# Attention and MLP on one core: row maxima turned by VectorE in 32 x 32 blocks and carried through DRAM instead of turned by TensorE

## The chip, the cores and the metric

One core of a Trainium2 chip runs the whole program. The metric is the device time of one execution in microseconds; of several executions the median is taken. The granted TensorE clock was 1.000 over the profiled execution.

## The reference

One transformer layer, sequence S = 2048, width D = 512, H = 32 heads of 16, MLP width F = 1792. First `h = x + softmax(q k^T / 4) v wo`, with q, k, v from `layernorm(x) @ wqkv`; then `h2 = h + silu(layernorm(h) @ w1) @ w2`:

```python
scores = jnp.einsum("bhqd,bhkd->bhqk", q, k) * scale
p = _softmax(scores, axis=-1)
o = jnp.einsum("bhqk,bhkd->bhqd", p, v)
...
h = x + _A_ref(_layernorm(x, axis=-1), A_wqkv, A_wo)
h2 = h + _B_ref(_layernorm(h, axis=-1), B_w1, B_w2)
```

The softmax needs the maximum of each query's 2048 scores before its exponentials can be taken.

## The kernel before

**Items and groups.** Attention is cut into 32 *items*: four heads by 512 queries each. Item i has 16 *groups* (one per 128 keys), so there are 512 groups, g = 16 i + c, walked in order by the main loop (L1244). A group is four score matmuls of 64 x 512 (`scores`, L451, keys as weights), each followed by an exponential on ScalarE (`pt<-ps`), and the four value matmuls in fp32 of the group two before (`values`, L815). Scores sit on one half of TensorE's rows, and between them stand up to three *maximum* matmuls on the other half (`maximum`, L273: 128 queries by 512 keys, 48 rows deep), each reduced over its 512 keys by VectorE (L289, `mx<-ps`). The maxima in group g serve items that come later; how many are done beside a group is decided by `maxima(g)` (L1221), normally three, two where c = 2.

**Where the other maxima are done.** An item has 64 maxima. Those of the first items are done beside the q, k, v projections; after each block of eight items (at g = 144, 272, 400, the `marks`) an MLP of the 512 finished rows runs as one piece (`mlp`, L1041), with *bursts* of maxima between its matmuls: pairs on both row halves, reduced two at a time (L287). Constants say how many: `BURSTS_1` in the first product, `BURSTS_2 = 16, 15, 13` bursts of four in the second, and `BESIDE = (138, 134, 106)` tells the planner the total per MLP. The last MLP stands after the last item.

**From maxima to scores.** When the last maximum of an item is recorded, `found_maxima` (L379) is called. `finish_max` (L296) takes the maximum over the four key blocks, either *urgent* by one VectorE reduction (L303, `nm<-mx`) or by six small GpSimd operations, and splits it in two halves of fp16 (`ns`, 128 queries x 32). `place_max` (L326) turns `ns` with a TensorE transpose into a PSUM bank of the ring `sm` (the three banks of the maxima), VectorE copies it out to `mt` (ScalarE before attention begins), and two DMAs of SyncE write `mt` to rows 48 and 49 of each half of the item's `qs`, so that the score matmuls subtract the maximum themselves. Scores of an item can't begin before that has landed.

**When.** `due_at` (L371) picks the step: where the item starts far enough ahead, the next group with c = 2 (`JOINT`; the previous item's result `pvs` is copied out of PSUM by VectorE there, L843); otherwise `WAIT` = 2 groups later. In the group that is due, `place_max` stands after the four scores and before the values (L1303). Outside attention, and near the marks, it is called by the agenda three steps later (`tick`, L356).

**Queues.** Each engine works through its instructions in program order, SyncE also: all DMAs here but the early weight loads are issued by SyncE, and a DMA that waits holds up those behind it. Per item SyncE carries eight loads of q and k for the item four ahead (L1250), the item's sums to DRAM and back (`dn`, `rc`, `dr`, `den`, L847 to L916) and, in the first items, weights to be split.

Of the kernel before, what the change touches and what calls it, by code (L numbers as in the profile page):

```python
# [12 lines left out]
F16 = mybir.dt.float16  # L13
# [7 lines left out]
P = 128  # L21
# [9 lines left out]
KC = S // P  # L31
# [21 lines left out]
RING = 5  # L53

HEADS = [(0, 1), (0, 0), (1, 1), (1, 0)]
ITEMS = NB * H // 4
# [5 lines left out]
FIRSTS = 8, 16, 24  # L62


WAIT = 2
JOINT = 2
AHEAD = 4


BESIDE = (138, 134, 106)  # L70
OUTPUT = 9

BESIDE_V = [(0, 0), (0, 4, 4, 4)], [(2, 2), (4, 4, 4, 4)], [(6, 6), (6, 6, 6, 6)]
# [5 lines left out]
BESIDE_A1 = 10, 9, 8, 7  # L79

BURSTS_1 = ({f: 6 for f in range(FC) if f not in (6, 13)},) * 2 + ({f: 6 for f in range(FC) if f % 3},)
BURSTS_2 = 16, 15, 13
SPAN_2 = 12 * (FC - 2)

MORE = 2, 2, 0
# [3 lines left out]
def attention_mlp_kernel(ctx: ExitStack, tc: tile.TileContext, x, wqkv, wo, w1, w2, out):  # L89
# [8 lines left out]
    def tr(*a):  # L98
        tc.keep_in_program_order(nc.tensor.transpose(*a))  # L99


    def pool(op, *a, **k):
        tc.keep_in_program_order(getattr(nc.gpsimd, op)(*a, **k))  # L103


    def pin(ins):
        tc.keep_in_program_order(ins)

    def act(fn, *a, **k):
        pin(getattr(nc.scalar, fn)(*a, **k))  # L110

    def dve(fn, *a, **k):
        pin(getattr(nc.vector, fn)(*a, **k))  # L113

    def dma(*a):
        pin(nc.sync.dma_start(*a))  # L116
# [22 lines left out]
    dram = ctx.enter_context(tc.tile_pool(name="dram", bufs=1, space=DRAM))  # L139
    small = ctx.enter_context(tc.tile_pool(name="small", bufs=3))  # L140
# [22 lines left out]
    def bank(kind="st", dtype=F32):  # L163
        ps = space[:, next_bank(kind), :]
        return ps if dtype == F32 else ps.bitcast(dtype)[:, :512]
# [32 lines left out]

    dn = dram.tile([H, 4, 512], F32, name="dn")
    dr = dram.tile([H, 4, 512], F32, name="dr")  # L200

    wd = {kind: dram.tile([FC, P, 2, 512], F16, name=f"{kind}d") for kind in ("w1", "w2")}

# [25 lines left out]
    ks, qs = [None] * RING, [None] * RING  # L229
# [37 lines left out]
    def start_of(piece):  # L267
        i, a = piece
        return KC * i + HALF * (a or 0)
# [3 lines left out]
    def maximum(i, kb, qt, a, j, n):  # L273

        piece = piece_of(i, a)
        width = 1 if i == LAST else 2
        if piece not in mx:
            mx[piece] = small.tile([P, 64], F32, name="mx", bufs=RING + 1)[:, :32 * width].rearrange(
                "p (j a q k) -> p j a q k", j=2, a=width, k=4)
            left[piece] = 32 * width  # L280
        heads = (0, 1) if j is None else (j,)
        for m, h in enumerate(heads):
            mm(space[:, n + m, :], qs[i % RING][64 * h:64 * h + 48, a, qt * P:qt * P + P],
               ks[i % RING][64 * h:64 * h + 48, a, kb * 512:kb * 512 + 512], start=True, stop=True)
        of = mx[piece][:, :, a % width, qt, kb]
        if j is None:
            pin(nc.vector.tensor_reduce(of, space[:, n:n + 2, :], axis=AX.X, op=ALU.max))  # L287
        else:
            pin(nc.vector.tensor_reduce(of[:, j:j + 1], space[:, n, :], axis=AX.X, op=ALU.max))  # L289
        left[piece] -= len(heads)  # L290
        at["done"] += len(heads)
        finish_rest()
        if left[piece] == 0:
            found_maxima(piece)

    def finish_max(piece, urgent):  # L296

        m4 = mx.pop(piece).rearrange("p j a q k -> p (j a q) k")
        rows = m4.shape[1]
        nm = small.tile([P, 16], F32, name="nm")[:, :rows]  # L300
        sign = 1.0
        if urgent:
            pin(nc.vector.tensor_reduce(nm, m4, axis=AX.X, op=ALU.max, negate=True))  # L303
        else:
            sign = -1.0
            m1, m2 = m4[:, :, :2], m4[:, :, 2:]
            for to, a, b in ((m2, m1, m2), (nm, m2[:, :, 0], m2[:, :, 1])):

                pool("tensor_tensor", to, b, a, ALU.subtract)
                pool("tensor_scalar", to, to, 0.0, None, op0=ALU.max)  # L310
                pool("tensor_tensor", to, to, a, ALU.add)
        ns = small.tile([P, 32], F16, name="ns")[:, :2 * rows]
        high, rest = (ns.rearrange("p (j r a) -> p j r a", j=2, r=2)[:, :, r, :] for r in range(2))
        nm = nm.rearrange("p (j a) -> p j a", j=2)
        pool("tensor_scalar", nm, nm, sign / MX, None, op0=ALU.mult)
        pool("tensor_copy", high, nm)
        pool("tensor_tensor", rest, nm, high, ALU.subtract)
        split[piece] = ns

    placed, split, unfinished, found_at = set(), {}, [], {"step": 0}  # L320

    def finish_rest():
        while unfinished:
            finish_max(unfinished.pop(), True)

    def place_max(piece):  # L326

        i, a = piece
        ns = split.pop(piece)
        n = ns.shape[1]  # L330
        ps = bank("sm", F16)
        tr(ps[:n, :P], ns, ident_h)
        mt = small.tile([32, P], F16, name="mt")[:n]
        if at["attention"]:
            dve("tensor_copy", mt, ps[:n, :P])
        else:
            act("copy", mt, ps[:n, :P])
        for j in range(2):
            dst = qs[i % RING][64 * j + 48:64 * j + 50, slice(None) if a is None else slice(a, a + 1)]
            dst = dst.rearrange("r a n -> r (a n)").rearrange("r (a b) -> r a b", b=P)  # L340
            pin(nc.sync.dma_start(dst, mt[n // 2 * j:n // 2 * (j + 1), :]))
        placed.add(piece)
# [6 lines left out]
    at = {"item": 0, "done": 0, "half": 0, "step": 0, "due": 0, "attention": False, "group": None, "ready": 0, "next": 0, "blocks": True}  # L349
    agenda, late = {}, {}  # L350

    def soon(steps, fn, *a):

        agenda.setdefault(at["step"] + steps, []).append((fn, a))
# [11 lines left out]
    def next_item():  # L366
        while at["item"] < ITEMS and not (todo[at["item"], 0] or todo[at["item"], 1]):
            at["item"] += 1
        return at["item"]

    def due_at(piece):  # L371

        g = at["group"]
        if g is None:
            return WAIT + 1
        joint = g + WAIT + (JOINT - g - WAIT) % KC
        return joint - g if joint < start_of(piece) - 2 and joint // KC - 1 not in (-1, *FIRSTS) else WAIT

    def found_maxima(piece):  # L379
        steps = due_at(piece)  # L380
        g = at["group"]
        if g is None or g + 1 in marks:
            soon(steps, place_max, piece)
            finish_max(piece, g is not None)
            return
        late.setdefault(at["step"] + steps, []).append(piece)
        if steps == WAIT:
            unfinished.append(piece)
            found_at["step"] = at["step"]
        else:  # L390
            finish_max(piece, False)

    def one_max(half=None, n=None):

# [32 lines left out]
    def burst(n, *pairs):  # L427
        assert n % 2 == 0
        for m in range(n // 2):
            two_max(pairs[m] if pairs else next_pair())  # L430
# [32 lines left out]
    with ExitStack() as pa:  # L463
# [320 lines left out]
        for g in range(1, NG // 2):  # L784
            for m, (b, key) in enumerate([(b, 1) for b in range(NB)] + [(b, 0) for b in range(NB)]):
# [3 lines left out]
                n = 8 * g + m - 12  # L789
# [251 lines left out]
    def mlp(b):  # L1041
# [9 lines left out]
        def some_scores(n):  # L1051
            for _ in range(n):
                scores(*ahead.pop(0), "sm")
# [22 lines left out]
        acc = []  # L1076
        inserts = {SPAN_2 * (n + 1) // BURSTS_2[b]: lambda: burst(4, 4, 6) for n in range(BURSTS_2[b])}
        inserts[12 * (FC - 2) + 8] = inserts[12 * (FC - 1) + 2] = lambda: some_scores(3)
# [140 lines left out]
    marks = [KC * (8 * b + 1) for b in range(1, NB)]  # L1219

    def maxima(g):  # L1221

        i, c = divmod(g, KC)
        goals = [(64 * (n + 1), KC * n) for n in range(i + 1, LAST)]
        goals += [(END - 32 * (1 - a), KC * LAST + HALF * a) for a in range(2) if KC * LAST + HALF * a > g]
        ready = min(ITEMS, i + RING - (0 if c == KC - 1 else 1)) * 64
        rate = max([(n - sum(x for x, m in zip(BESIDE, marks) if g <= m <= start) - at["done"])
                    / max(1, start - AHEAD - g) for n, start in goals] or [0])
        if ready < END:
            rate = min(rate, (ready - at["done"]) / (KC - 1 - c or KC))  # L1230
        at["due"] += max(0, rate)
        if g < LAG or g in marks or g - 1 in marks:

            return 0
        at["ready"] = ready
        most = 2 if c == JOINT and i and i - 1 not in FIRSTS else 3
        n = max(0, min(most, int(at["due"]), ready - at["done"]))
        at["due"] -= n
        return n
# [4 lines left out]
    for g in range(groups):  # L1244
        tick()
        i, c = divmod(g, KC)
# [13 lines left out]
        if i in FIRSTS:  # L1260
            b, n = i // 8 - 1, c - OUTPUT
# [20 lines left out]
        if g == 1:  # L1282
            dve("memset", pv, 0.0)
        at["group"] = g
        n = maxima(g)

        half = 1 - head(g, g % 2)[1]
        j = next_item()
# [58 lines left out]
```

## Time and profile before

| what | value |
|---|---|
| median of 3 runs | 1611.84 us (1611.49 to 1612.39) |
| profiled execution, its own time | 1613.29 us |
| profiled execution, span from first to last instruction | 1611.5 us |
| TensorE matmuls busy | 1590.8 us, 99% |
| VectorE busy | 1392.9 us, 86% |
| ScalarE busy | 1210.3 us, 75% |
| GpSimd busy | 456.4 us, 28% |
| granted TensorE clock | 1.000 |

A row of the timeline gives the start in us from the span's beginning, the duration, the engine, the line of the kernel, the operation, what it writes and reads, the partitions and elements, and how many equal instructions follow each other; in brackets the engine's idle time ahead of it and what ended it. Value matmuls (`ps<-pt,va`) come once per group, eight records of them, so the distance of two such rows is the time of one group. Line 96 is the helper through which all matmuls go, line 99 that of transposes, lines 103, 110, 113 and 116 those of GpSimd, ScalarE, VectorE and DMA issues.

### The profile page before, as it was taken

The numbers are of one execution on the slowest core, as the hardware profiler recorded it, in microseconds if no ns is written. First come the engines' busy times: TensorE is split into PE (matmuls) and PEld (weight loads), VectorE is DVE, ScalarE is ACT, GpSimd is POOL, SyncE is SP. The second block draws the span as 40 slices with busy tenths as digits, with TensorE's granted clock in tenths as the row PEclk, the third lists the DMA queues.
The fourth block names the chain that finished last, engine by engine and source line by source line (L and its number), as shares of the span: only waits on it lengthen the run. The fifth ranks groups of instructions, "written<-read, shape, count | busy, mean of one in ns | idle before, by whom it ended". The sixth has DMA issues, their size and how long they took to land.

```text
span 1611.5 us, 28300 instructions
## 1 busy us (share of the span) xinstructions
PE 1590.8 (99%) x10553; PEld 477.9 (30%) x10553; DVE 1392.9 (86%) x2060; ACT 1210.3 (75%) x2387; POOL 456.4 (28%) x702
## 2 busy tenths in 40 slices
PE   9999999999999999999999999999999999999998
PEld 6433222222233322222233322222233322222253
DVE  7899999999989889999989889999976789999421
ACT  6545799999964179999964179999964089999732
POOL 4743544544326101211136101211126101111100
PEclk9999999999999999999999999999999999999999
DMA  5668533342322111121223211121123111100222
GB/s 194 181 162 234 139 85 90 110 140 85 101 63 99 60 52 33 37 60 33 51 73 99 60 52 33 38 59 33 50 75 108 50 52 38 33 11 22 73 85 72
DMA packets 100949, 125.89 MB, mean 78 GB/s; under 512 B 24144, under 2 KB 61072, under 8 KB 100812
## 3 DMA queue, kind: packets, MB, share of 16 engines
q1 hardware_dynamic: 96204, 115.71, 25.1%
q10 hardware_dynamic: 4608, 8.39, 1.9%
q8 instruction: 82, 1.34, 0.3%
q14 instruction: 55, 0.45, 0.1%
HBM read 93.45 MB, written 24.63 MB: 73 GB/s over the span
## 4 chain that ended last, share of the span: by engine, by line
PE 85%; DVE 6%; ACT 4%; DMA 2%; issue 1%; POOL 1%; SPq 1%; DVEq 0%; ACTq 0%; POOLq 0%
PE ps L96 84%; ACT pt L110 4%; DVE mx L289 2%; DVE mx L287 2%; PE ps L99 1%; DMA qd<-sh 1%; DVE ot L113 1%; SPq L116 1%; DMA qs<-mt 0%; DVE st L113 0%; DMA ks<-in_A_x_dram 0%; DVE htl L113 0%; DVE hx L113 0%; POOL ri L103 0%; DVE pvs L113 0%
## 5 line engine op out<-in xcount | busy, mean ns | idle before, releaser
L110 ACT ACTIVATE pt<-ps 128x512 f32<-128x512 f32 x2048 | 1011.3, 631 | 154.9 <-PE ps L96 153.4
L289 DVE TENSOR_REDUCE mx<-ps 128x1 f32<-128x512 f32 x1474 | 926.8, 683 | 44.9 <-PE ps L96 16.1
L96 PE MATMUL ps<-qs,ks 64*128 64x512 f16 x2048 | 533.6, 379 | 5.8 <-DMA qs<-mt 2.5
L96 PE MATMUL ps<-pt,va 128*17 128x512 f32 x4096 | 537.5, 598 | 0.6
L96 PE MATMUL ps<-ks,qs 48*128 48x512 f16 x2048 | 494.7, 380 | 1.8 <-DVE mx L287 1.8
L287 DVE TENSOR_REDUCE mx<-ps 128x2 f32<-128x1024 f32 x287 | 334.0, 1219 | 55.1 <-PE ps L96 54.1
L96 PEld LDWEIGHTS <-ks 64*128 64x128 f16 x2048 | 150.8, 95 | 553.0 <-issue 433.2
L103 POOL TENSOR_TENSOR ri<-rc,minus 128x16 f32<-128x16 f32 x31 | 90.7, 2925 | 294.8 <-DMA rc<-dn 294.8
L96 PE MATMUL ps<-w,gh 128*128 128x512 f16 x672 | 157.4, 380 | 0.5 <-ACT g L110 0.4
L96 PEld LDWEIGHTS <-qs 48*128 48x128 f16 x2048 | 125.1, 94 | 75.3 <-issue 61.9
L96 PE MATMUL ps<-hth,w 128*128 128x512 f16 (+1 forms) x472 | 132.9, 369 | 0.0
L96 PEld LDWEIGHTS ps<-pt,va 128*17 128x17 f32 x4096 | 68.9, 95 | 214.6 <-issue 201.1
L110 ACT ACTIVATE g<-ps,factors 128x512 f32<-128x512 f32 x56 | 38.6, 689 | 124.6 <-PE ps L96 102.9
L96 PEld LDWEIGHTS <-w 128*128 128x128 f16 x708 | 66.1, 98 | 79.1 <-issue 11.8
L103 POOL TENSOR_TENSOR mx<-mx 128x32 f32<-128x32 f32 x36 | 8.6, 239 | 281.8 <-DVE mx L289 216.6
L96 PEld LDWEIGHTS <-gh 128*128 128x128 f16 x672 | 61.1, 98 | 85.5 <-issue 19.8
L96 PE MATMUL ps<-htl,w 128*128 128x512 f16 (+1 forms) x236 | 83.9, 368 | 0.0
L103 POOL TENSOR_SCALAR nm<-nm 128x16 f32<-128x16 f32 (+1 forms) x51 | 12.9, 254 | 169.8 <-DVE nm L303 154.5
L110 ACT ACTIVATE ks<-ps 128x512 f32<-128x512 f32 x30 | 18.0, 599 | 50.3 <-PE ps L96 37.6
L113 DVE SCALAR_TENSOR_TENSOR gh<-g,factors,gh 128x512 f16<-128x512 f32 x14 | 10.5, 751 | 52.2 <-ACT gh L110 52.2
L103 POOL TENSOR_TENSOR sl<-ks,sh 128x512 f16<-128x512 f32 x30 | 35.3, 1178 | 52.9 <-ACT sh L110 38.5
L103 POOL TENSOR_TENSOR gh<-g,gh 128x512 f16<-128x512 f32 x42 | 48.5, 1154 | 3.5
(153 smaller groups left out, 983.5 us busy)
## 6 DMA issues: line engine op xcount, KB each, us to landing
ks<-kd SPq DMA_DIRECT2D x120, 192.0 KB
w<-w1d SPq DMA_DIRECT2D x56, 256.0 KB
w<-w2d SPq DMA_DIRECT2D x56, 256.0 KB
ks<-in_B_w_dram ACTq DMA_DIRECT2D x28, 256.0 KB
w<-in_B_w_dram SPq DMA_DIRECT2D x28, 256.0 KB
qs<-qd SPq DMA_DIRECT2D x128, 48.0 KB
kd<-sh SPq DMA_DIRECT2D x16, 256.0 KB
qd<-sh SPq DMA_DIRECT2D x16, 256.0 KB
```

The source lines that it names most:

```text
L96: tc.keep_in_program_order(nc.tensor.matmul(*a, **k))
L99: tc.keep_in_program_order(nc.tensor.transpose(*a))
L103: tc.keep_in_program_order(getattr(nc.gpsimd, op)(*a, **k))
L110: pin(getattr(nc.scalar, fn)(*a, **k))
L113: pin(getattr(nc.vector, fn)(*a, **k))
L116: pin(nc.sync.dma_start(*a))
L287: pin(nc.vector.tensor_reduce(of, space[:, n:n + 2, :], axis=AX.X, op=ALU.max))
L289: pin(nc.vector.tensor_reduce(of[:, j:j + 1], space[:, n, :], axis=AX.X, op=ALU.max))
```

## The change

A second way to place an item's maxima, `place_far`, is added. `ns` (128 x 32) is turned by one VectorE transpose, which works on blocks of 32 x 32: row 32 b + c of `mt` then holds column c for the queries 32 b to 32 b + 31. Four DMAs write the four blocks side by side into a DRAM tensor `md` (32 x 128 per item, 64 bytes at a time), and two DMAs read it back, 16 rows of it as two rows of 1024, into the item's `qs`. `found_maxima` takes this way outside attention, near the marks, and for every whole item that starts more than `FAR` = 8 groups later; inside attention it is called `CALM` = 6 steps later, at the head of a group, and the maximum over key blocks is then always taken by GpSimd. Other items go as before, two groups later, with VectorE's urgent reduction; `due_at` is gone. In a group that is to hold a TensorE transpose, at most two maxima are done. The third MLP has 14 bursts in its second product instead of 13, and the planner is told 110 instead of 106.

In the instruction streams of the two built kernels this comes to: TensorE transposes of `ns` 33 before, 6 after; VectorE block transposes 0 and 27, copies of `mt` 30 and 6 (`mn`), urgent reductions 13 and 4; ScalarE copies of `mt` 3 and 0; small GpSimd operations 54 more; SyncE DMAs 108 more. Single reductions 1474 and 1482, pairs 287 and 283.

```diff
+FAR = 8
+CALM = 6
-BESIDE = (138, 134, 106)
+BESIDE = (138, 134, 110)
-BURSTS_2 = 16, 15, 13
+BURSTS_2 = 16, 15, 14
...
+    md = dram.tile([ITEMS, 32, P], F16, name="md")
...
+    def place_far(piece):
+        i, _ = piece
+        mt = small.tile([P, 32], F16, name="mt")
+        dve("transpose", mt, split.pop(piece))
+        for b in range(4):
+            dma(md[i, :, 32 * b:32 * b + 32], mt[32 * b:32 * b + 32, :])
+        for j in range(2):
+            dma(qs[i % RING][64 * j + 48:64 * j + 50].rearrange("r a n -> r (a n)"),
+                md[i, 16 * j:16 * j + 16, :].rearrange("(r q) n -> r (q n)", r=2))
+        placed.add(piece)
...
-        mt = small.tile([32, P], F16, name="mt")[:n]
-        if at["attention"]:
-            dve("tensor_copy", mt, ps[:n, :P])
-        else:
-            act("copy", mt, ps[:n, :P])
+        mt = small.tile([32, P], F16, name="mn", bufs=1)[:n]
+        dve("tensor_copy", mt, ps[:n, :P])
...
-    def due_at(piece):
-        g = at["group"]
-        if g is None:
-            return WAIT + 1
-        joint = g + WAIT + (JOINT - g - WAIT) % KC
-        return joint - g if joint < start_of(piece) - 2 and joint // KC - 1 not in (-1, *FIRSTS) else WAIT
-
-    def found_maxima(piece):
-        steps = due_at(piece)
+    def found_maxima(piece):
         g = at["group"]
-        if g is None or g + 1 in marks:
-            soon(steps, place_max, piece)
-            finish_max(piece, g is not None)
+        marked = g is not None and g + 1 in marks
+        if g is None or marked or piece[1] is None and start_of(piece) - g > FAR:
+            soon(WAIT + 1 if g is None or marked else CALM, place_far, piece)
+            finish_max(piece, marked)
             return
-        late.setdefault(at["step"] + steps, []).append(piece)
-        if steps == WAIT:
-            unfinished.append(piece)
-            found_at["step"] = at["step"]
-        else:
-            finish_max(piece, False)
+        late.setdefault(at["step"] + WAIT, []).append(piece)
+        unfinished.append(piece)
+        found_at["step"] = at["step"]
...
-        most = 2 if c == JOINT and i and i - 1 not in FIRSTS else 3
+        most = 2 if at["step"] in late or c == JOINT and i and i - 1 not in FIRSTS else 3
```

## The prediction

> **What bounds the kernel now.** I read the page first, then the timeline of TensorE, group by group, then VectorE, GpSimd and SyncE at the places where the change acts.
>
> ```profile
> PE 1590.8 (99%) x10553; PEld 477.9 (30%) x10553; DVE 1392.9 (86%) x2060; ACT 1210.3 (75%) x2387; POOL 456.4 (28%) x702
> PEclk9999999999999999999999999999999999999999
> PE 85%; DVE 6%; ACT 4%; DMA 2%; issue 1%; POOL 1%; SPq 1%; DVEq 0%; ACTq 0%; POOLq 0%
> ```
>
> TensorE is busy 99% of the span at full clock, and the chain that ends last runs 85% through it. So a microsecond taken from TensorE, or from its waits, counts. What one transpose costs there is read not from its own duration, since matmuls overlap, but from the distance of its neighbours. Value matmuls come once per group, so two such rows are one group apart.
>
> ```profile
> L113 DVE COPY mt<-ps x30: 197/200/213, 215.8 to 1494.1; 32x128 f16<-32x128 f16 x28, 16x128 f16<-16x128 f16 x2
> 1107.12 1.05 PE L96 MATMUL ps<-pt,va 128*17 128x512 f32 x8
> 1109.08 1.05 PE L96 MATMUL ps<-pt,va 128*17 128x512 f32 x8
> 1111.27 0.22 PE L99 MATMUL ps<-ident_h,ns 128*32 128x128 f16 x1 [0.16 <-DVE mx L289]
> 1111.28 1.06 PE L96 MATMUL ps<-pt,va 128*17 128x512 f32 x8
> 1097.26 1.05 PE L96 MATMUL ps<-pt,va 128*17 128x512 f32 x8
> 1099.28 1.05 PE L96 MATMUL ps<-pt,va 128*17 128x512 f32 x8
> 1065.84 1.05 PE L96 MATMUL ps<-pt,va 128*17 128x512 f32 x8
> 1067.86 1.05 PE L96 MATMUL ps<-pt,va 128*17 128x512 f32 x8
> ```
>
> The time of a group is very regular: 1.96 us (1107.12 to 1109.08). The group with the transpose at 1111.27 takes 2.20, 0.24 more; the transpose waits for the bank of a maximum, as its bracket says. At c = 2 a group takes 2.02 without a transpose (1097.26 to 1099.28) and 2.02 with one (1065.84 to 1067.86): there the values wait for VectorE's copy of `pvs`, and the transpose costs nothing. So of the transposes in attention only those away from c = 2 are worth anything.
>
> **The change part by part.** The sum is a difference: durations come from the profiled execution, whose span is 1611.5 us and whose own time is 1613.29; I take it from the median, 1611.84. Which item goes which way is counted through the two programs' loops: 27 of 33 pieces go far; items 8, 16, 24, 30 and the halves of 31 stay with TensorE.
>
> (1) *Single transposes away from c = 2 that go:* items 6, 7, 15, 23, 29. 5 x 0.24 = **1.2 us less**. Those that stood at c = 2 give nothing.
>
> (2) *Urgent reductions that go:* VectorE's `nm<-mx` in attention costs TensorE nothing or a tenth, by where it falls.
>
> ```profile
> 1108.11 0.39 PE L96 MATMUL ps<-qs,ks 64*128 64x512 f16 x1
> 1108.41 0.21 DVE L303 TENSOR_REDUCE nm<-mx 128x16 f32<-128x64 f32 x1
> 1151.23 0.21 DVE L303 TENSOR_REDUCE nm<-mx 128x16 f32<-128x64 f32 x1
> 1150.54 1.05 PE L96 MATMUL ps<-pt,va 128*17 128x512 f32 x8
> 1152.61 1.05 PE L96 MATMUL ps<-pt,va 128*17 128x512 f32 x8
> ```
>
> The one at 1108.41 stands ahead of a group's first reduction, and its group (1107.12 to 1109.08) is not longer. The one at 1151.23 stands ahead of a group's last reduction: 2.07 instead of 1.96, 0.11 more. Of those that go, items 6, 7, 14, 15 and 28 are of the costly kind: 5 x 0.11 = **0.55 less**. GpSimd gets nine times six small operations; it is busy 28% and has six groups for them, nothing.
>
> (3) *VectorE's block transposes come.* The trace has none. Lower bound nothing; nearest rows are the copy of `mt` and `nm<-mx`, 0.20 and 0.21 us, on as many values; I take 0.2. In attention they stand at the head of a group, exactly where the 0.21 us reduction cost nothing. Two fall in a group c = 1, ahead of the `pvs` copy: between 0 and 0.11 each, **0.1 more** together. The Trainium skill, "VectorE: DVE Perf Modes", section "The three transpose paths", gives 311 ns for VectorE on 128 x 128 bf16, and says that it turns 32 x 32 blocks only; by 0.31 instead of 0.2 the term would be 0.2. No run here shows it yet.
>
> (4) *The way through DRAM.* Four stores, a wait until they have landed, two loads.
>
> ```profile
> 383.41 0.33 SPq L116 DMA_DIRECT2D dr<-ri  x1
> 385.24 0.84 SPq L116 DMA_DIRECT2D den<-dr  x2
> 710.20 0.35 SPq L116 DMA_DIRECT2D rc<-dn  x1
> 711.83 2.93 POOL L103 TENSOR_TENSOR ri<-rc,minus 128x16 f32<-128x16 f32 x1 [8.52 <-DMA rc<-dn]
> ```
>
> A store of 64-byte pieces and the load behind it are 1.83 us apart (383.41 to 385.24), two issues take 0.84, a small load is used 1.63 after its issue (710.20 to 711.83). The block transpose ends about 0.5 us into its group (the reduction at 1108.41 starts 0.30 after its group's first scores at 1108.11). So: last store issued at 0.5 + 3 x 0.42 = 1.8, loads at 3.6 and 4.05, landed at 5.7, or 5.9 if the load is like a `qs<-mt` (below). Items 7 and 23 have the least time: found at c = 7 of the item before, called six groups later, 3 groups = 5.88 us ahead of their first scores. Items 15 and 29 have 4 groups, 7.84, the others more. I take 0.1 for each of 7 and 23, **0.2 more**; bounds 0 and 1.2 each (chain of 7.1). The Trainium skill, "DMA: Bandwidth & Descriptors", section "Anatomy of one DMA — SWDGE (gpsimd) path", puts about 2.0 us fixed on each DMA, mostly the write receipt, for GpSimd's queue; at 2.0 for each hop the chain would be 6.25 and the term 0.75. The store's row, 1.83, speaks for less.
> SyncE is held for some 4 us per item. Behind it stand loads of q and k for the item four ahead, weights loaded five ahead, and `pvs` sums that only GpSimd awaits: nothing.
>
> (5) *Items that stay, with two maxima in the transpose's group.*
>
> ```profile
> 428.83 0.20 DVE L113 COPY mt<-ps 32x128 f16<-32x128 f16 x1
> 429.06 1.38 SPq L341 DMA_DIRECT2D qs<-mt  x2
> 429.75 1.05 PE L96 MATMUL ps<-pt,va 128*17 128x512 f32 x8
> 432.61 1.05 PE L96 MATMUL ps<-pt,va 128*17 128x512 f32 x8
> 425.80 3.11 DVE L289 TENSOR_REDUCE mx<-ps 128x1 f32<-128x512 f32 x5
> ```
>
> Item 8: the copy to `mt` runs behind the group's third reduction, its DMAs land about 1.8 us after the second issue, and the group after takes 2.86 (429.75 to 432.61): 0.9 of waiting. Items 24 and 30 are the same. With two maxima the copy comes one reduction earlier, 0.6 us (3.11 for five): 3 x 0.6 = 1.8 less. For item 24 the urgent reduction moves to a free place (0.11 less), for item 30 to a dear one (0.11 more). The first half of item 31 saves 0.15 of its 0.24, since the transpose finds a free bank. Item 16 loses: one maximum fewer at item 8 makes it complete a group later, so that it is placed two groups ahead instead of three and has a wait of 0.3, and a dear reduction of 0.11. Together **1.5 less**; bounds 0.5 and 3.
>
> (6) *Transposes beside projections and MLPs.*
>
> ```profile
> 1217.74 0.38 PE L96 MATMUL ps<-htl,w 128*128 128x512 f16 x1
> 1218.05 0.23 PE L99 MATMUL ps<-ident_h,ns 128*32 128x128 f16 x1
> 1218.21 0.60 PE L96 MATMUL ps<-hth,w 128*128 128x512 f16 x2
> 492.24 1.18 PE L96 MATMUL ps<-ks,qs 48*128 48x512 f16 x6
> 493.35 0.61 PE L96 MATMUL ps<-hth,w 128*128 128x512 f16 x2
> 529.12 1.46 PE L96 MATMUL ps<-w,gh 128*128 128x512 f16 x6 [0.23 <-ACT g L110]
> 167.47 6.91 DVE L287 TENSOR_REDUCE mx<-ps 128x2 f32<-128x1024 f32 x6 [0.16 <-PE ps L96]
> ```
>
> Two matmuls with a transpose between them start 0.47 apart (1217.74 to 1218.21); without one 0.22, since two take 0.60 together and one 0.38: 0.25 for a transpose. Three in the MLPs and two in the projections save that; one that follows value matmuls, 0.2; a burst of six behind the first MLP's one takes 1.11 (492.24 to 493.35), where a burst of four adds 0.63 (term 8) and one pair more 0.22: some 0.3 over its kind, since its bank waits for the copy of `mt`. Two between the MLP's products save nothing, as TensorE waits there for ScalarE's `g` (529.12), nor does the third in the projections, where VectorE is the chain (167.47). 5 x 0.25 + 0.2 + 0.3, **1.8 less**; bounds 0.8 and 2.6.
>
> (7) *Behind the first and second MLP.*
>
> ```profile
> 577.05 0.61 PE L96 MATMUL ps<-w,gh 128*128 128x512 f16 x2
> 578.07 0.22 PE L99 MATMUL ps<-ident_h,ns 128*32 128x128 f16 x1 [0.42 <-ACT pt L110]
> 578.22 0.39 PE L96 MATMUL ps<-qs,ks 64*128 64x512 f16 x1
> 1297.66 0.61 PE L96 MATMUL ps<-w,gh 128*128 128x512 f16 x2
> 1298.20 0.39 PE L96 MATMUL ps<-qs,ks 64*128 64x512 f16 x1
> ```
>
> Here the transpose waits for an exponential that holds its bank: 1.17 us from the last pair to the scores, 0.54 behind the third MLP, which has none. 0.63 goes, but VectorE's queue is full here, so I take 0.5 each: **1.0 less**; bounds 0.3 and 1.26.
>
> (8) *The burst more.*
>
> ```profile
> 1255.35 1.24 PE L96 MATMUL ps<-w,gh 128*128 128x512 f16 x5
> 1257.06 1.25 PE L96 MATMUL ps<-w,gh 128*128 128x512 f16 x5
> ```
>
> Five matmuls and a burst take 1.71, without it five times 0.215 ((1.24 - 0.38) / 4) = 1.08: **0.63 more**. Maxima left out beside attention give nothing back, since four scores set that half of a group with two maxima or three.
>
> Sum: 1.2 + 0.55 + 1.5 + 1.8 + 1.0 = 6.05 less, 0.1 + 0.2 + 0.63 = 0.93 more: **5.1 us less, 1606.7 us**.
>
> **The rivals.**
> *The way through DRAM is late (slower).* Mechanism: the scores of items 7, 23, 15 and 29 wait for `qs<-md`. A chain of T us costs 2 (T - 5.88) + 2 (T - 7.84). At T = 8.2 it eats the gain (4.6 + 0.7); at T = 10 it costs 12.6 instead of 0.2, and the time is 1619. For it: pieces of 64 bytes, six DMAs in line, k loads of 192 KB just ahead of them. Against: a pair of hops is 1.83 + 1.63 us in the rows.
> *Other engines keep the gain outside attention (same).* VectorE has the chain in part of the projections, and an MLP step of three pair reductions leaves it no room; terms 6 and 7 go, 2.3 less: 1609.5.
> *The short-notice wait goes altogether (faster still).* If the copy, no longer behind the third reduction, starts early enough that scores don't wait, term 5 is 3 instead of 1.5 and term 7 its upper bound: 1604.9.
> *The change doesn't do what it says:* the instruction streams exclude it, 27 transposes go.
>
> **How the numbers follow.** Forecast 62%, late DRAM 10%, gain kept by others 14%, wait gone 14%. About 0.2%, 3.2 us, is what a measurement of this kernel can tell from no change. Faster by more: 0.62 + 0.14 = 0.76; same 0.14; slower 0.10. The range takes in the third and second case and the bounds of terms 4 to 7, 1604.0 to 1611.0, and leaves out late DRAM and some of the rest.
>
> **What would show it.** Groups with one transpose between 1.96 neighbours gone (1, 2); 1.96 kept where a block transpose stands (3); the first scores of items 7 and 23 waiting for `qs<-md` or not (4); the groups ahead of items 8, 24 and 30 at 2.3 instead of 2.86, and a new wait ahead of item 16 (5); steps of the MLPs without 0.25 (6); 0.6 behind two MLPs (7); the third MLP longer by one burst (8). Wrong would make it a landing time over 2.5 us on either hop, or block transposes far over 0.2 us.

## The result, and the profile after

| | before | after |
|---|---|---|
| median | 1611.61 us (1611.35 to 1612.61, 17 runs) | 1608.22 us (1607.40 to 1611.74, 17 runs) |
| profiled execution, its own time | 1613.29 us | 1611.74 us |
| its span | 1611.5 us | 1609.9 us |
| its granted TensorE clock | 1.000 | 0.998 |

The changed kernel takes 0.9979 of the time of before [0.9972, 0.9986]: 3.4 us less, faster by about what a measurement of this kernel can tell. Forecast were 5.1 us less, 1606.7 with a range from 1604.0 to 1611.0.

Two things stand in the way of reading that difference from the two spans. The profiled execution of after is the longest of its 17 runs. And the first 60 us, which hold no changed instruction, differ by up to 2 us between profiled executions. So I compare group with group: group g is key block g mod 16 of item g div 16 (both from 0), and its time runs from its first score to the next group's. Where nothing acts on a group, its time agrees to 0.01 us in every profile of this study.

The page of after, in the parts that answer to those of before: busy time, and the shares of the chain that ended last.

```profile
PE 1588.4 (99%) x10526; PEld 476.3 (30%) x10526; DVE 1391.9 (86%) x2058; ACT 1208.2 (75%) x2384; POOL 470.0 (29%) x756
PE 71%; ACT 19%; DVE 6%; DMA 2%; issue 1%; POOL 1%; SPq 0%; ACTq 0%; DVEq 0%; POOLq 0%
```

27 matmuls are gone (10553 to 10526), TensorE is busy 2.4 us less and VectorE 1.0 us less, and the share of TensorE is still 99%. The chain now passes more through ScalarE, but that engine is busy 75%: TensorE remains the one that is full.

**Single transposes and block transposes.** TensorE in the two groups of before that stood around 1109, now without a transpose, and VectorE's block transposes as the view of the tile `mt` has them (min/median/max in ns):

```profile
1106.80 1.05 PE L98 MATMUL ps<-pt,va 128*17 128x512 f32 x8
1108.76 1.05 PE L98 MATMUL ps<-pt,va 128*17 128x512 f32 x8
L115 DVE STREAM_TRANSPOSE mt<-ns x27: 199/201/205, 117.0 to 1409.7; 128x32 f16<-128x32 f16 x27
```

The group takes 1.96 (1106.80 to 1108.76). A block transpose takes 0.20 each time, and every group inside attention that has one takes 1.96.

**The way through DRAM, where it is late.** TensorE ahead of the first scores of item 7 (397.47) and of item 15 (761.15), then VectorE and SyncE for item 7:

```profile
394.99 0.39 PE L98 MATMUL ps<-qs,ks 64*128 64x512 f16 x1
397.47 0.39 PE L98 MATMUL ps<-qs,ks 64*128 64x512 f16 x1 [0.45 <-ACT pt L112]
761.15 0.39 PE L98 MATMUL ps<-qs,ks 64*128 64x512 f16 x1 [0.77 <-DMA qs<-md]
```
```profile
391.37 0.20 DVE L115 STREAM_TRANSPOSE mt<-ns 128x32 f16<-128x32 f16 x1
```
```profile
391.60 2.58 SPq L118 DMA_DIRECT2D md<-mt  x4
395.73 0.52 SPq L118 DMA_DIRECT2D qs<-md  x2
```

Item 7's scores come 2.48 after the scores of the group before (394.99 to 397.47) instead of 1.96: 0.52 late. The bracket names ScalarE's `pt`, which came at almost the same moment; that it is the load shows in the run below in which the transposes start earlier and nothing else is changed, where this wait is gone. The four stores need 2.58 here where four issues of 0.42 would need 1.7, and the loads are issued 4.13 after the first store. Item 15 comes 0.84 late (its group takes 2.80). Items 23 and 29, with the same leads, wait for nothing.

**The last half of item 31.** TensorE, then SyncE:

```profile
1495.32 1.05 PE L98 MATMUL ps<-pt,va 128*17 128x512 f32 x8
1498.17 0.78 PE L98 MATMUL ps<-qs,ks 64*128 64x512 f16 x4 [1.80 <-DMA qs<-mn]
1498.88 1.77 PE L98 MATMUL ps<-pt,va 128*17 128x512 f32 x8
```
```profile
1491.11 1.38 SPq L118 DMA_DIRECT2D w<-w1d  x3
1492.53 0.43 SPq L118 DMA_DIRECT2D w<-w2d  x1
1493.06 1.39 SPq L354 DMA_DIRECT2D qs<-mn  x2
```

This piece stays with TensorE in both kernels. In after its two small DMAs stand right behind 1 MB of weights for the last MLP, and the scores begin 4.4 us after the second issue, where item 8 had its rows in 1.8; they wait 1.80 us. Behind the wait TensorE runs at half clock, as the eight value matmuls at 1498.88 show (1.77 for 1.05). In before the scores did not wait, though the two DMAs stood behind the same four loads. There they were issued 4.1 us before their scores were due, in after 3.2 us, since `ot<-pvs` ahead of them took 3.30 instead of 2.56; and in after they were used 5.1 us after the first issue, so that they landed at least 1 us later as well. In this execution that costs 2.65 us in groups 503 to 506; in other executions it ran from 0 to 1.1.

### The profile page after: what moved, and what is told of

It is laid out like the page before. It is cut to its first block, busy times and chain, and to the rows that moved or that the text cites. A ratio compares the mean times of both kernels' runs of the same rounds, so it can differ in the third digit from the quotient of the medians.

```text
span 1609.9 us, 28386 instructions
## 1 busy us (share of the span) xinstructions
PE 1588.4 (99%) x10526; PEld 476.3 (30%) x10526; DVE 1391.9 (86%) x2058; ACT 1208.2 (75%) x2384; POOL 470.0 (29%) x756
## 4 chain that ended last, share of the span: by engine, by line
PE 71%; ACT 19%; DVE 6%; DMA 2%; issue 1%; POOL 1%; SPq 0%; ACTq 0%; DVEq 0%; POOLq 0%
PE ps L98 70%; ACT pt L112 18%; DVE mx L293 2%; DVE mx L291 1%; PE ps L101 1%; DMA qd<-sh 1%; DVE ot L115 1%; DMA qs<-mn 1%; DVE pvs L115 0%; DVE htl L115 0%; SPq L118 0%; DVE st L115 0%; POOL rs L105 0%; DVE hx L115 0%; POOL ri L105 0%
## 5 line engine op out<-in xcount | busy, mean ns | idle before, releaser
L291 DVE TENSOR_REDUCE mx<-ps 128x2 f32<-128x1024 f32 x283 | 329.9, 1219 | 53.3 <-PE ps L98 52.2
L105 POOL TENSOR_TENSOR mx<-mx 128x32 f32<-128x32 f32 x54 | 13.0, 240 | 402.3 <-DVE mx L293 395.8
L98 PEld LDWEIGHTS <-w 128*128 128x128 f16 x708 | 66.3, 98 | 80.0 <-issue 12.4
L98 PE MATMUL ps<-xth,wqk_l 128*128 128x512 f16 x120 | 45.5, 379 | 0.8 <-DVE wqk_l L115 0.7
```

Of the source, the lines that this page charges most:

```text
L98: tc.keep_in_program_order(nc.tensor.matmul(*a, **k))
```

## The experiments

All were compared with the kernel before on the same chip, whose medians there were 1611.55 to 1611.82 us. A ratio is to that kernel, with its 95% interval. None of them leaves out or changes a part of the computation.

**The changed kernel again,** to have its waits from a second execution.

> The changed kernel itself once more, as the measure for the next three on the same chip. Theory A (waits of scores for DMAs make the shortfall, and they differ from execution to execution): a median 2.5 to 4.5 us under the kernel before, runs spread over 1.5 us or more while those of before stay within 1 us; in the profile the waits ahead of items 7 and 15 (0.5 and 0.8 us before) and at the last half item (1.8 us) come in other sizes or at other items. Theory B (the shortfall is a fixed cost of the new instructions): the same waits of the same size again, and a spread like that of before.

1608.43 us (1606.87 to 1610.03, 11 runs), 0.998 [0.9971, 0.9989]. The waits vary from execution to execution: item 7 0.50 late, item 15 1.02, the last half 0.77 and no half clock. Everything else is as in the first profile to 0.01 us.

**Block transposes three groups earlier in attention.**

```diff
-CALM = 6
+CALM = 3
```

> CALM = 3: the block transpose and the six DMAs of each item in attention come three groups (5.9 us) earlier; nothing else changes. Theory A: the groups ahead of items 7, 15, 23 and 29 take 1.96 us, no score waits for a load from DRAM, and the median is 0.7 to 1.4 us under the changed kernel's, about 1607. Rival: the waits come from SyncE's queue being full whatever the lead, and move to other items or to q and k loads: no gain, or a block transpose that waits for GpSimd's halves and holds VectorE: slower by 1 us or more.

1607.84 us (1606.83 to 1608.74, 9 runs), 0.9976 [0.9966, 0.9986]. The waits ahead of items 7 and 15 are gone, all other groups but those at the last half are as they were. The first scores of the group before item 7 and of item 7, now without a bracket and 1.96 apart:

```profile
395.93 0.39 PE L98 MATMUL ps<-qs,ks 64*128 64x512 f16 x1
397.89 0.39 PE L98 MATMUL ps<-qs,ks 64*128 64x512 f16 x1
```

The loads of items 7 and 15 are issued 7.4 and 3.8 us ahead of their scores here. So those waits are the way through DRAM. One profile could be luck: with `CALM` = 6 item 15 is 0.84 to 1.04 late in four of seven profiles of this study and in time in three, item 7 late by 0.1 to 0.5 in six. With `CALM` = 3 neither is late in any of three. In the median it brings 0.6 us, less than the 1.4 to 1.5 of the two waits; the intervals overlap, and the last half still waited 1.18 in its profile.

**Weights of the last MLP two groups later.**

```diff
-            if c == 4:
+            if c == 6:
                 for f in range(3):
                     load_weights("w1", f)
```

> The 1 MB of weights for the last MLP is asked for two groups later (c = 6 instead of 4 of the last item), so that it stands behind the last item's maxima on SyncE's queue instead of ahead of them. Theory A: the wait of the last half item for its maxima (1.8 us in the profile of the changed kernel) and the half clock for 3.4 us behind it don't occur in any run; median up to 1 us lower, the highest run under 1610. Rival: the long runs come from elsewhere (the way through DRAM), and the spread stays as it is; or the weights come too late for the last MLP, which then starts later by up to 2 us.

1607.81 us (1607.01 to 1608.83, 11 runs), 0.9974 [0.9965, 0.9983]. Group 503 has its 1.96 again, and no run is above 1608.83, where after had runs up to 1611.74. Over the whole study the two small DMAs stand behind these loads in nine profiles, the kernel before among them, and the scores of the last half wait in six of the nine (0.4 to 1.9 us). In four they stand ahead of the loads (three with the loads later; in the fourth, the rule of two taken back, the item completes earlier), and the scores wait in none. That speaks for the queue of weights ahead of the two small DMAs; one kernel alone wouldn't show it, since three of the nine go without the wait. Items 7 and 15 are still late here, by 0.26 and 1.04.

**Block transposes two groups later,** to price the way through DRAM where it must be late.

```diff
-CALM = 6
+CALM = 8
```

> CALM = 8: the block transpose and its six DMAs come two groups later, so that items 7 and 23 have one group (1.96 us) and items 15 and 29 two (3.92 us) ahead of their scores. Theory A (the way through DRAM takes about 5.1 us from the head of its group and is paid as soon as the lead is shorter): waits of some 3.1 us ahead of items 7 and 23 and 1.2 to 2 ahead of 15 and 29, 7 to 8 us more than the changed kernel; if a wait of over 1.8 us halves the clock behind it, as the end of its profile showed, 1 to 1.7 us more for each such wait: 1616 to 1620. Rival (waits come from a full queue, not from the lead): items 23 and 29, which did not wait before, still don't, and the time stays under 1611.

1620.63 us (1620.41 to 1620.85, 4 runs), 1.0052 [1.0035, 1.0069], 0.6 above the range that I expected. Item 7 in it, on TensorE, VectorE and SyncE; then its granted clock by stretch (us from to, length, busy PE, PEld, DVE, ACT, POOL with counts, clock, DMA share, GB/s):

```profile
399.49 0.60 PE L98 MATMUL ps<-qs,ks 64*128 64x512 f16 x1 [2.98 <-DMA qs<-md]
```
```profile
394.78 0.20 DVE L115 STREAM_TRANSPOSE mt<-ns 128x32 f16<-128x32 f16 x1
```
```profile
395.01 1.69 SPq L118 DMA_DIRECT2D md<-mt  x4
397.83 0.52 SPq L118 DMA_DIRECT2D qs<-md  x2
```
```profile
399.00:405.70 6.70, 6.21 (x26) 1.17 (x30) 3.77 (x6) 3.98 (x8) 2.46 (x3) 0.50 0.13 39
405.70:408.00 2.30, 2.23 (x22) 0.35 (x14) 1.56 (x4) 1.43 (x4) 0.00 (x0) 0.99 0.00 0
1132.80:1136.20 3.40, 3.40 (x16) 0.56 (x15) 2.26 (x5) 2.44 (x6) 0.00 (x0) 0.50 0.00 0
```

Here SyncE is free, and the chain can be read undisturbed: transpose at 394.78, first store 0.23 later, the fourth some 1.27 after that (1.69 for four), the load 1.55 after the fourth, the scores 1.66 after the first load's issue: 4.7 us from transpose to scores, 5.0 from the head of the group (394.48). Items 7 and 23 have one group, 1.96, and wait 3.05 and 3.07; items 15 and 29 have two, 3.92, and wait 1.33 and 1.47. Those four are 8.9 us. Behind the waits of 3 us the clock is at 0.50, for 6.8 us once and 3.4 us once, which adds 2.75 and 1.44 in the groups that follow; behind the waits of 1.33 and 1.47 it is not. With 1.0 more ahead of item 24, and less the 1.4 to 1.5 that items 7 and 15 wait at CALM = 6, that makes 12.6 us, and 12.2 to 12.4 were measured (1620.63 to the two medians of after). So the late-DRAM rival has its mechanism, and at CALM = 6 items 7 and 23 have 0.9 us to spare (5.88 less 5.0) as long as SyncE is free.

**The rule of two maxima alone taken back.**

```diff
-        most = 2 if at["step"] in late or c == JOINT and i and i - 1 not in FIRSTS else 3
+        most = 2 if c == JOINT and i and i - 1 not in FIRSTS else 3
```

> The rule of three maxima also in the group of a TensorE transpose is put back, all else as in the changed kernel. Theory A: groups 126 and 382 take 2.21 and the ones behind them 2.86 again (0.6 and 0.7 us more), the first half of item 31 0.25 to 0.3 more; items 16 and 30, complete a group earlier, lose their waits (0.4 each less). Net 0.9 us slower, 1609. Rival (the two maxima are worth nothing in themselves, since the maxima left out return elsewhere): within 0.3 us of the changed kernel.

1608.42 us (1608.15 to 1609.64, 10 runs), 0.9979 [0.9969, 0.9988]: the median of after, so my expectation for the whole missed. Group by group the rule is worth what was said: items 8 and 24 are 0.59 and 1.08 slower without it, item 16 gains 0.42, item 30 0.30, and the first half of item 31 loses 0.39. But the maxima pair up differently in the first MLP (0.44 more), which with 0.1 in the second makes 1.9 more. Against that, this profile lacks what the profile of after again had in waits: 0.3 of item 7's 0.5, item 15's 1.0 and the last half's 0.7, together 2.0. That the absent waits belong to the edit and not to the execution isn't shown.

**The third MLP's burst taken back.**

```diff
-BESIDE = (138, 134, 110)
-BURSTS_2 = 16, 15, 14
+BESIDE = (138, 134, 106)
+BURSTS_2 = 16, 15, 13
```

> The third MLP has 13 bursts again, the planner is told 106. The MLP gets 0.64 us shorter. Theory A: the four maxima are missing ahead of item 30, which completes a group later (477 instead of 476), is placed one group ahead of its scores and makes them wait about 2.5 us instead of 0.5; net 1.3 us slower or more (a wait of that length may halve the clock): 1609.5 to 1611. Rival (the burst is only a cost): 0.6 us faster, 1607.6.

1611.0 us (1608.9 to 1612.94, 10 runs), 0.9994 [0.9984, 1.0004]: by the medians 2.6 to 2.8 slower than after, though the intervals (0.9972 to 0.9986 and 0.9971 to 0.9989 there) still overlap a little. The third MLP is 0.65 shorter, as expected, but item 30 pays. TensorE ahead of its first scores:

```profile
1448.93 0.39 PE L98 MATMUL ps<-qs,ks 64*128 64x512 f16 x1 [2.49 <-DMA qs<-mn]
1450.28 1.91 PE L98 MATMUL ps<-pt,va 128*17 128x512 f32 x8
```

Without the burst's four maxima item 30 completes one group later, its scores wait 1.98 us more (group 479: 4.46 for 2.48), and the clock falls behind it (1.91 for eight values), another 1.4 over the next three groups. So the burst, which the prediction counted only as 0.63 us more, buys item 30's lead.

**Outside attention the old way, inside the new.**

```diff
-            soon(WAIT + 1 if g is None or marked else CALM, place_far, piece)
+            soon(WAIT + 1 if g is None or marked else CALM, place_max if g is None or marked else place_far, piece)
```

> Items that complete outside attention (ten of them, beside projections, MLPs and at the marks) are turned by TensorE again, two groups or three steps later; in attention as in the changed kernel. Theory A: three times 0.255 us in the projections, 0.7 in the first MLP, 0.5 in the third, nothing in the second, and only 0.1 behind each of the first two MLPs, where VectorE's last row sum holds the scores with or without the transpose: 2.1 us slower, 1610.4. Rival (as predicted: 0.5 behind each MLP): 2.9 us slower or more.

1612.67 us (1611.97 to 1614.16, 10 runs), 1.0006 [0.9996, 1.0015]: 4.2 to 4.5 slower than after, twice what I expected. The projections lose their 0.7; the first MLP loses 2.3, the second 0.9, the third 1.5, and item 24 waits 0.4 more. That is 5.8; against it, this profile lacks the waits of items 7 and 15, 1.4. TensorE in a step of the first MLP's second product:

```profile
528.06 0.82 PE L98 MATMUL ps<-w,gh 128*128 128x512 f16 x3
530.37 0.22 PE L101 MATMUL ps<-ident_h,ns 128*32 128x128 f16 x1 [1.48 <-DVE mx L291]
530.51 1.47 PE L98 MATMUL ps<-w,gh 128*128 128x512 f16 x6
```

Item 8 has one maximum fewer by the rule of two, so later items complete a step later, and there the transpose's bank belongs to a burst whose maxima VectorE hasn't taken: it waits 1.48 us, and the step takes 5.4 us where it took 3.6. A transpose in that place costs anything from 0 to 1.8 us, by where it falls among the bursts.

**Before, with only its pieces outside attention the new way.**

```diff
-            soon(steps, place_max, piece)
+            soon(WAIT + 1, place_far, piece)
```

> The kernel before with one part of the change alone: items that complete outside attention go the way through DRAM, ten of them; everything in attention, the number of bursts and the maxima per group stay as before. Theory A, from the profiles so far: three times 0.255 us in the projections less 0.07, 0.7 to 0.85 in the first MLP, 0 in the second, 0.5 in the third, 0.1 behind each of the first two: 2.0 to 2.2 us faster, 1609.5. Rival (the far way is worth only what it does in attention): within 0.7 us of before; rival as predicted at first (0.5 behind each MLP): 2.8 faster.

1609.95 us (1609.44 to 1610.53, 10 runs), 0.9989 [0.998, 0.9999]: 1.9 less than before. The projections give 0.70 and the MLPs 0.48, -0.27 (a loss) and 0.73. Behind the first and second MLP 0.63 and 0.74 go and 0.54 comes back each time, which is nearly the same as in after. Its profile also has 0.4 and 0.8 of new waits ahead of item 24 and at the last half; the sum of the groups agrees with the median, 1.9 less, only without these two.

**Behind the first two MLPs, the two single maxima moved out of VectorE's way,** to a burst of two near the start of the second product.

```diff
             scores(*ahead.pop(0))
             scores(*ahead.pop(0), "sm")
-            if b < 2:
-                singles(2)
...
+        if b < 2:
+            inserts[3] = lambda: burst(2, 4)
```

> The changed kernel with the two single maxima behind the last matmuls of the first and second MLP moved to the head of the second product, as a pair. Theory A (VectorE's two reductions ahead of the MLP's last row sum, 0.6 us each, hold the bank that the scores behind the MLP need; the transpose only stood in the same gap): the groups 145, 146 and 273, 274 lose 0.85 us per MLP, the pair costs 0.1 to 0.2, so 1.3 to 1.5 us less than the changed kernel, about 1606.9. Rival (something else holds the scores there): no gain, 1608.3 or more.

1606.84 us (1605.87 to 1607.16, 5 runs), 0.9967 [0.9954, 0.998]. Groups 145 and 146 take 3.22 and 2.44 for 3.44 and 3.09 in after, 273 and 274 the same: 0.87 less for each MLP, and 0.1 more in the first MLP. The third MLP with the groups behind it, where nothing was moved, is 0.2 shorter. By the medians it is 1.4 to 1.6 less than after, as expected. Lines of this place stand below, at point (7).

**The three together:** transposes earlier, weights later, single maxima moved.

> CALM = 3, the later weights, and the two single maxima behind the last matmuls of the first and second MLP moved to the head of the MLP's second product, as a pair. Theory A: no wait ahead of items 7 and 15, none at the last half item, and the groups behind the two MLPs (3.44 and 3.09 us) shorter by 0.5 us each, as the last row sum of the MLP no longer stands behind two reductions on VectorE; a pair more in the second product costs 0.22 us each: 1606 to 1606.8, all runs within 1 us. Rival (what is freed is waited for again): 1607.5 or more.

1605.11 us (1604.72 to 1606.40, 5 runs), 0.9959 [0.9946, 0.9973], 0.9 below the range that I expected.

> The same kernel as best, to narrow its interval: 1604.7 to 1606.4 again if its gain lies in waits that are gone and not in a lucky execution; single runs up to 1608 if a wait for a DMA is still left at some item.

1604.88 us (1604.71 to 1605.61, 5 runs), 0.9957 [0.9943, 0.9971]. By the medians it is 6.4 to 6.9 us below the kernel before and 3.3 below the changed one; none of the three waits (items 7, 15, the last half) is in either profile.

## Why the prediction was right or wrong, point by point

The direction was right, and the size was 1.7 us too large. (The upper end of the range, 1611.0, is not the sum that I called it: terms 4 to 7 all at their worst bounds give 1611.6.) By its own steps, from the group times of the profile after against those of before, in us:

| term | predicted | measured |
|---|---|---|
| (1) single transposes | -1.2 | -1.24 |
| (2) urgent reductions | -0.55 | -0.58 |
| (3) block transposes | +0.1 | 0.0 |
| (4) way through DRAM | +0.2 | +1.36 |
| (5) items that stay | -1.5 | -1.72 |
| (6) projections and MLPs | -1.8 | -1.92 |
| (7) behind two MLPs | -1.0 | -0.2 |
| (8) the burst | +0.63 | +0.64 |
| not foreseen: last half of item 31 | | 0 to +2.65 |

Without the last row the measured terms sum to -3.7; what the prediction hadn't named (0.11 gained in groups 497 to 499, 0.23 lost in the last MLP, which isn't in the diff) makes it -3.5. The medians differ by 3.4. The waits of (4) and of the last row vary between executions, so this agrees about as well as it can.

**(1), (2), (3) right in their sizes.** The five groups 83, 105, 232, 360 and 456 lost 0.246 to 0.250 each, the five with a dear reduction 0.106 to 0.128. The block transposes cost nothing even in the groups c = 1, where I had allowed 0.1. Of the two rows that I had taken as nearest, only the copy has as many values; the urgent reduction reads twice as many. The 311 ns that the Trainium skill, "VectorE: DVE Perf Modes", section "The three transpose paths", gives for a tile of 128 x 128 did not decide here: 0.20 for 128 x 32.

**(4) The step that failed most: the chain of four stores and two loads, taken at 5.7 to 5.9 us with SyncE free, and "nothing" for GpSimd's small operations and for SyncE's queue.** The chain itself is shorter, 5.0 from the group's head (1.55 from store to load where I took 1.83). But SyncE isn't free. GpSimd and SyncE ahead of item 15, in after and then in before:

```profile
742.54 0.24 POOL L105 TENSOR_TENSOR mx<-mx 128x32 f32<-128x32 f32 x1 [31.06 <-DVE mx L293]
749.33 0.34 SPq L118 DMA_DIRECT2D dr<-ri  x1
750.81 1.69 SPq L118 DMA_DIRECT2D den<-dr  x4
752.54 1.44 SPq L118 DMA_DIRECT2D ks<-kd  x1
755.01 1.76 SPq L118 DMA_DIRECT2D md<-mt  x4
758.83 0.52 SPq L118 DMA_DIRECT2D qs<-md  x2
```
```profile
745.80 0.26 POOL L103 TENSOR_SCALAR nm<-nm 128x16 f32<-128x16 f32 x1 [29.98 <-DVE nm L303]
750.61 0.34 SPq L116 DMA_DIRECT2D dr<-ri  x1
```

SyncE issues nothing for 10.7 us ahead of `dr<-ri`, which waits for GpSimd's `ri`, made from an earlier item's sums. What piles up behind it, sums and loads of q and k, is issued until 754.9. GpSimd does `ri` after item 15's small operations. These begin within 0.15 us of the head of group 231 in both kernels, but with six more of them `dr<-ri` comes 6.8 after their start (742.54 to 749.33) instead of 4.8 (745.80 to 750.61). Besides, one load of k took 1.44 to issue, where the others take 0.42. So item 15's block transpose is done at 752.98, and its first store stands 2.5 us into the group instead of 0.5; the loads come 3.8 behind that store, where the run with `CALM` = 8 has 2.8, and the scores 2.3 behind the loads, where it has 1.7. In the run again it was the four `den<-dr` that took 3.08 instead of 1.7. In all six profiles with `CALM` = 6 and 27 block transposes the first store of item 15 stands 1.6 to 2.6 us behind its transpose. At item 7 it is 0.23, and there one of the four stores itself took 1.31 to issue. That item 15 would be in time without the 2 us of the six operations is worked out from these rows; no run takes them away alone.

So two items of four are late: item 7 by 0.52, inside the bounds that I gave but not at the end that I chose, and item 15 by 0.84, which with 2 us to spare I had at nothing. I had priced what the new DMAs hold up, and not what holds them up; and I had asked whether GpSimd has room for six more operations, not what stands behind them. Why one issue takes an extra microsecond, and why at other places of the queue in other executions, stays open.

**(5) right,** piece by piece: item 8 -0.59 (I had -0.6), item 24 -0.73 (-0.71), item 30 -0.49 (-0.49), item 16 +0.41 (+0.41), first half of item 31 -0.31 (-0.15). TensorE around item 8:

```profile
425.93 0.23 PE L101 MATMUL ps<-ident_h,ns 128*32 128x128 f16 x1
425.94 1.08 PE L98 MATMUL ps<-pt,va 128*17 128x512 f32 x8
427.93 1.05 PE L98 MATMUL ps<-pt,va 128*17 128x512 f32 x8
430.40 1.05 PE L98 MATMUL ps<-pt,va 128*17 128x512 f32 x8
```

The group after the transpose takes 2.47 (427.93 to 430.40), for 2.86 before, where I had said 2.3. The transpose's own group gives 0.21 beside it (2.00 for 2.21), which I hadn't split off; the 0.6 of the sum are both.

**(6) right in sum.** Two matmuls that had a transpose between them start 0.22 apart:

```profile
1214.46 0.38 PE L98 MATMUL ps<-htl,w 128*128 128x512 f16 x1
1214.68 0.59 PE L98 MATMUL ps<-hth,w 128*128 128x512 f16 x2
```

The third transpose of the projections, which I took for hidden behind VectorE, saved its 0.255 as well. In the second MLP the one between the products saved nothing, as predicted.

**(7) The other step that failed, by 0.8: "0.63 goes".** It goes and comes back. Behind the first MLP, after, on TensorE and VectorE:

```profile
574.11 0.61 PE L98 MATMUL ps<-w,gh 128*128 128x512 f16 x2
574.64 0.39 PE L98 MATMUL ps<-qs,ks 64*128 64x512 f16 x1
575.34 0.38 PE L98 MATMUL ps<-qs,ks 64*128 64x512 f16 x1
576.21 0.37 PE L98 MATMUL ps<-qs,ks 64*128 64x512 f16 x1 [0.49 <-DVE ot L115]
576.75 0.62 PE L98 MATMUL ps<-pt,va 128*17 128x512 f32 x4
```
```profile
574.21 1.29 DVE L293 TENSOR_REDUCE mx<-ps 128x1 f32<-128x512 f32 x2
575.41 0.74 DVE L115 SCALAR_TENSOR_TENSOR ot<-ps,factors,ot 128x512 f32<-128x512 f32 x1
576.07 0.20 DVE L115 STREAM_TRANSPOSE mt<-ns 128x32 f16<-128x32 f16 x1
```

The first scores now stand 0.53 behind the last pair (574.11 to 574.64), just as behind the third MLP. But two scores later TensorE waits for VectorE's last row sum `ot`, which stands behind two single reductions: group 145 is 0.63 shorter and group 146 0.53 longer. The transpose's wait lay beside that one. I had read the bracket that ended last in before, and not asked what was due right after it. The run with the two reductions moved shows it (TensorE, then VectorE):

```profile
573.13 0.61 PE L98 MATMUL ps<-w,gh 128*128 128x512 f16 x2
574.58 0.37 PE L98 MATMUL ps<-qs,ks 64*128 64x512 f16 x1 [0.30 <-DVE ot L115]
575.12 1.05 PE L98 MATMUL ps<-pt,va 128*17 128x512 f32 x8
```
```profile
573.77 0.75 DVE L115 SCALAR_TENSOR_TENSOR ot<-ps,factors,ot 128x512 f32<-128x512 f32 x1 [0.30 <-PE ps L98]
```

These lines are from the second run of the three together, whose times of these groups are those of the single edit. `ot` starts when TensorE has written its sum, and the values come 1.99 behind the last pair (573.13 to 575.12) instead of 2.64 (574.11 to 576.75).

**(8) right in its price,** 0.64, and incomplete: its four maxima also buy item 30 a group, without which the kernel was 2.6 us slower by the medians.

**The rivals.** The wait that goes altogether didn't happen: item 8 still waits 0.45. Other engines keeping the gain holds for term (7) alone. Late DRAM is real but reaches two items by 0.5 to 1.0 and not all four by more; the run with the transposes two groups later gives it in full.

## What to carry to other kernels

When transfers are moved off an engine that is full, reckon the queue that they join in both directions: what they hold up, and what may hold them up, here a microsecond or two that in part comes and goes between executions; a lead with one microsecond to spare, or even nearly three, is not yet a lead. When work is moved to an engine with room, ask what stands behind it there: six small operations on GpSimd put off a DMA for which the whole queue waited. When a wait goes, look for the next one on the same engine within the same microsecond before counting it, since the bracket of a profile names only the one that ended last. And where an edit changes how many pieces of work are done by a certain place, count who completes later for it: the burst that cost 0.64 us saved item 30 a wait of 2 us and the half clock behind it.

## What the runs showed of the hardware

**TensorE's clock falls behind a wait of under 2 us.** Windows of after, just ahead of the wait and behind it:

```profile
1494.00:1496.00 2.00, 1.93 (x16) 0.34 (x12) 0.14 (x1) 2.00 (x5) 1.92 (x2) 1.00 0.96 348
1500.00:1502.00 2.00, 2.00 (x12) 0.29 (x12) 0.00 (x0) 1.43 (x4) 0.00 (x0) 0.50 0.38 86
```

The granted clock is 1.00 ahead of the wait of 1.80 us and 0.50 behind it, for 3.41 us. The same came behind the 2.49 of the run with the burst taken back and behind both waits of 3 us of the run with late transposes (once for twice as long), and behind none of 1.5 us or less. The Trainium skill, "TensorE: Matmul & The Clock Gate", section "Part 1: The HAM clock gate", has the clock judged by free-running windows of 3413 ns and halved after an idle one. The length at half clock agrees, 3.41 us. The free-running windows agree too: in the trace's record of the granted clock the four stretches at half clock inside attention begin 437 (after), 423 (burst taken back), 115 and 330 (late transposes) times 3.413 us behind the clock's first rise. That a whole window must be idle doesn't agree: in the 3.41 us ahead of these four TensorE sat idle for 1.80, 2.49, 2.39 and 2.45 us, and of all other such windows inside attention none has over 1.45 us. Idle time alone isn't shown to be the rule, since a window with 1.98 us idle at the very end of the run with pieces outside attention the old way was followed by full clock.

**A small DMA behind large ones lands late.** In after the two rows of `mn` were used 4.4 us after their second issue behind four weight loads, with the DMA engines busy 96% (window 1494 to 1496 above); at item 8 it was 1.8 us. Behind the same loads in before they had landed within 3.4 us, so the order of the queue alone doesn't fix the delay. A single issue can also be held. The view of the tile `md` has the issue times (min/median/max in ns):

```profile
L118 SPq DMA_DIRECT2D md<-mt x108: 302/419/1307, 122.3 to 1411.2; - x108
```

One of the 108 stores took 1.31 us to issue, three times the median.
